# The planned transfer rate, column halves and whole tiles of group 0 in a linear-attention and feed-forward kernel

## Chip, cores and metric

The program runs on one NeuronCore of a Trainium2 chip. The metric is the device time of one execution in microseconds (us); lower is better. Everything is float32 at the interface.

## What is computed

```python
f = 1.0 / (1.0 + np.exp(-f_logit))                     # q, k, v, f_logit: (4, 8, 768, 48)
for t in range(S):
    state = f[:, :, t, :, None] * state + einsum('bhd,bhe->bhde', k[:, :, t], v[:, :, t])
    y[:, :, t] = einsum('bhd,bhde->bhe', q[:, :, t], state)
x = y.transpose(0, 2, 1, 3).reshape(3072, 384)
h = x @ w_in                                           # (384, 2048)
g = h * np.tanh(np.log1p(np.exp(h)))
return g @ w_out                                       # (2048, 384)
```

## The kernel before

**Tiling.** The recurrence is worked chunk by chunk: 24 chunks of 128 time steps of one batch, each by a few small matmuls with a state that is carried along. Four chunks make a group of 512 tokens; there are six groups (g = 0 to 5). The feed-forward part takes a group through 16 tiles of d_ff (j = 0 to 15): `moe_in` gives h of one tile (128 x 512), `mish` turns it into g on ScalarE and VectorE, `moe_out` adds its share to the three output banks o. Groups 0 and 1 are worked in an interleaved order (`units`), so that each half of the weights is loaded once.

**Two precisions of matmul.** As a rule a tile is worked in split form: the operands are split into a high and a low part of type float32r (`split_w`, `split_x`, the last two steps of `mish`), and three products of the parts stand for one, nine matmuls for h (L227) and nine for o (L265). The first tiles of group 0 (j < `WHOLE`) are worked whole instead: plain float32 matmuls, three for h (L235) and three for o (L238), with nothing to split at that point; the weights of such a tile are split later, at its turn in group 1.

**Column halves.** The first `EARLY_J` tiles of group 0 are worked in two halves of 256 tokens: first the halves that need only chunks 0 and 1, then those that need chunks 2 and 3.

**Weights.** The weights of tile j come as one transfer of 768 KB into one of two buffers `raw` (in two pieces of 384 KB each while transfers are "early"), 8 bytes to a pair of numbers, and are put together by L374 on ScalarE and L376, L377, L379 on VectorE. Below, w0 is the weights of tile 0, w2 those of tile 2. A chunk's input comes as two transfers of 512 KB, lk and qv.

**Transfers.** All transfers are issued by SyncE's queue in the order of the plan. The first 32 pieces are paced (`fetch`): each waits until an earlier one has landed, so that at most 1200 KB are under way.

**Order.** Every step is recorded with `Plan.add` (engine, estimated cost in ns, the resources that it reads and writes), and `Plan.order` looks for an order: for each setting (`ahead`, `haste`) it packs the steps by list scheduling, forward and backward in turn, and keeps the packing with the earliest estimated end. `Plan.pack` estimates when a transfer lands: transfers go one after the other at 0.32 KB per ns. Each engine's instructions are then issued in order of their estimated start, and run in that order: an instruction that waits holds up all behind it on its engine. `Plan.issue` fills estimated gaps of TensorE up to the first feed-forward output with matmuls on zeros (L361, `idle`), which count as busy in the profile but compute nothing.

Lines that the steps below touch: L374 to L379 put weights together; L391 and L392 split them; L251, L243, L254, L255 (ScalarE) and L252, L256, L247 (VectorE) are steps of `mish`; L613 and L618 copy a chunk's output and spread the fourth head pair's rows with three matmuls; L503, L517, L476, L560, L572, L584 are the matmuls of the recurrence.

Of the kernel before, what the change touches and what calls it, by code (L numbers as in the profile page):

```python
# [39 lines left out]
PACED = 16  # L40
FLIGHT = 1200
EARLY = 24
EARLY_J = 3
WHOLE = 4


class Plan:
# [26 lines left out]
    def pack(self, rank, ahead, haste, back=False):  # L74


        steps = self.steps
        count = len(steps)
        engine, cost, port = [s[0] for s in steps], [s[1] for s in steps], [s[5] for s in steps]
        before = [s[3] for s in steps]  # L80
        after = [[] for _ in steps]
        for i in range(count):
            for b in before[i]:
                after[b].append(i)
        if back:
            before, after = after, before
        free = dict.fromkeys(self.FREE, 0.0) if back else dict(self.FREE)
        queue = {e: [] for e in free}
        left, ready, start = [len(b) for b in before], [0.0] * count, [0.0] * count
        for i in range(count):  # L90
            if not left[i]:
                queue[engine[i]].append(i)
        transfers = shared = 0.0
        for _ in range(count):
            best = None
            for e, q in queue.items():
                if q:
                    at = [(max(ready[i], shared) if port[i] else ready[i], i) for i in q]
                    t0 = max(free[e], min(at)[0])
                    _, t, i = min(  # L100
                        (rank[i] + haste * max(0.0, r - t0), max(free[e], r), i)
                        for r, i in at if r <= t0 + ahead
                    )
                    if best is None or t < best[0]:
                        best = t, i
            t, i = best
            e = engine[i]
            queue[e].remove(i)
            start[i] = t
            end = free[e] = t + cost[i]  # L110
            if port[i]:
                shared = end
            if e == "sp" and not back:
                transfers = max(transfers, end + 650.0) + steps[i][4] / 0.32
                end = transfers - 650.0
            for a in after[i]:
                f = a if back else i
                if engine[i] == engine[a] == "pe":
                    lag = 0.0
                else:  # L120
                    lag = self.LATENCY[engine[f]]
                    if back and engine[f] == "sp":
                        lag += steps[f][4] / 0.32
                ready[a] = max(ready[a], end + lag)
                left[a] -= 1
                if not left[a]:
                    queue[engine[a]].append(a)
        return start

    def order(self):  # L130
        count = len(self.steps)
        cost = [s[1] for s in self.steps]
        best = None
        for ahead, haste in ((0.0, 0.0), (100.0, 1.0), (100.0, 20.0), (300.0, 20.0), (600.0, 20.0)):
            rank = list(range(count))
            for _ in range(10):
                start = self.pack(rank, ahead, haste)
                end = max(start[i] + cost[i] for i in range(count))
                if best is None or end < best:
                    best, self.start = end, start  # L140
                back = self.pack([-start[i] - cost[i] for i in range(count)], ahead, haste, True)
                rank = [-back[i] - cost[i] for i in range(count)]
        return sorted(range(count), key=lambda i: (self.start[i], i))
# [34 lines left out]
def recurrence_moe_kernel(  # L178
# [89 lines left out]
    with tc.tile_pool(name="work", bufs=1) as pool, tc.tile_pool(  # L268
# [113 lines left out]
        def split_w(j):  # L382
            w, kw = (first[j], ("first", j)) if j < HF else (wt_[j % 2].bitcast(F32), ("wt", j % 2))
            old = [[], []]
            if j >= HF:
                old = [
                    [k for n in held for x in inputs(n)[0] for k in x]
                    + [("s", ("xt", 0, c), t) for c in range(GC) for t in range(NP)],
                    [("first", i) for i in range(HF)],
                ]  # L390
            add("act", T_ACT(W_TILE), lambda: nc.scalar.activation(weights(j)[0], w, AF.Copy), [kw], [("w", "h", j)] + old[0])  # L391
            add("dve", T_DVE(W_TILE), lambda: nc.vector.tensor_tensor(  # L392
                weights(j)[1], w, weights(j)[0].bitcast(F32), ALU.subtract), [kw, ("w", "h", j)],
                [("w", "l", j)] + old[1], port=True)

        def split_x():
            x = xt_[0]
            for a in range(NK):
                ks, kh, kl = ([(z, ("xt", 0, c), a) for c in range(GC)] for z in "shl")
                add("act", T_ACT(GT), lambda a=a: nc.scalar.activation(x[:, 0, a], xs[:, a], AF.Copy), ks, kh)  # L400
                add("dve", T_DVE(GT), lambda a=a: nc.vector.tensor_tensor(
                    x[:, 1, a], xs[:, a], x[:, 0, a].bitcast(F32), ALU.subtract), ks + kh, kl, port=True)
# [256 lines left out]

        units = [(0, j, x) for x in range(2) for j in range(EARLY_J)] + [(0, j, 2) for j in range(EARLY_J, HF)]  # L660
        units += [(1, j, 2) for j in range(HF)] + [(g, j, 2) for g in range(2) for j in range(HF, NF)]
# [3 lines left out]
        def attend_goal(u):  # L665

            per = 4 * GC
            u = u // 2 if u < 2 * EARLY_J else u - EARLY_J
            if u < NF + HF:
# [17 lines left out]
        def out_unit(u):  # L687
# [13 lines left out]
            if u == 0:  # L701
                plan.until = len(plan.steps)
            if g == 0 and j < WHOLE:
                for m in range(NK):
# [26 lines left out]
        for u in range(len(units) + LAG):  # L731
            if u < len(units):
                g, j, part = units[u]
                whole = g == 0 and j < WHOLE
                if g == 0 and part != 1:
                    load_w(j)
                    if not whole:
                        split_w(j)
                if u == EARLY_J + WHOLE:
                    split_x()  # L740
                if g == 1 and j < WHOLE:
                    split_w(j)
# [129 lines left out]
def _layout(q, k, v, f_logit, moe_w_in, moe_w_out):  # L872
# [18 lines left out]
    for a in range(NK):  # L891
        for e in range(2):
            for r in range(16):
                order += [head_at(a, e) * D + 3 * r + m for m in range(3)]
                order.append(head_at(NP - 1, e) * D + 3 * r + a)
    w_in = moe_w_in[np.array(order)].reshape(NK, P, NF, P).transpose(2, 1, 0, 3)
    ww = np.empty((NF, P, 2, NK, P), dtype=moe_w_in.dtype)
    ww[:, :, 0] = w_in
# [33 lines left out]
```

## Time and profile before

| | us |
|---|---|
| median of 3 runs (506.26 to 507.40) | 507.32 |
| profiled execution, its own time | 506.54 |
| its span (first to last instruction) | 504.7 |
| TensorE busy in the span | 490.8 (97%) |
| VectorE, ScalarE, GpSimd busy | 334.7, 356.8, 147.8 |

The profile names PE (TensorE's matmuls), DVE (VectorE), ACT (ScalarE), POOL (GpSimd) and SP (SyncE); L12 is line 12 of the kernel. Two things help in reading it. A plain float32 matmul leaves two records, a float32r one leaves one, so "L235 x6" is three matmuls. And the end of a matmul is modelled and overlaps the start of the next, so that costs of matmuls are best taken from start to start; the same holds in a smaller way on ACT and DVE, where the next instruction starts about 0.1 us before the shown end.

### The profile page before, as it was taken

To read this page: it belongs to the slowest core of one execution; us is meant where nothing else is said; L and a number is where in the kernel's file an instruction comes from. 1 tells how busy PE (TensorE), PEld (TensorE's weight loads), DVE (VectorE), ACT (ScalarE), POOL (GpSimd) and SP (SyncE) were. 2 spreads that over 40 slices of the span, in tenths; PEclk is the share of its full clock that TensorE was granted. 3 is DMA by queue.
4 is the path that set the end of the run, shared out by engine and by line. 5 is a ranking of instruction groups with operands and counts; after the bars stand their busy time and mean duration, and the time that the engine had idled before them with its cause. 6 is when DMAs were issued, how large, how long until landed. Compare 5 with 4: busy or idle time off the path is not lost.

```text
span 504.7 us, 12824 instructions
## 1 busy us (share of the span) xinstructions
PE 490.8 (97%) x5352; PEld 396.0 (78%) x5352; DVE 334.7 (66%) x588; ACT 356.8 (71%) x681; POOL 147.8 (29%) x128
## 2 busy tenths in 40 slices
PE   9779999999999999999999999999999999999995
PEld 8668767788888777787887887888788878878884
DVE  4679999998856874876666756656776453534341
ACT  6769999999976774867667766775776654655561
POOL 0411211100014343344333443443242323332422
PEclk9999999999999999999999999999999999999999
DMA  7875555651300634311221411121230000010001
GB/s 251 266 239 205 196 207 201 218 181 62 126 0 22 202 116 150 113 43 46 83 75 43 147 43 43 64 86 53 83 108 1 2 12 22 24 39 1 0 1 68
DMA packets 17105, 48.47 MB, mean 96 GB/s; under 512 B 2000, under 2 KB 2000, under 8 KB 17040
## 3 DMA queue, kind: packets, MB, share of 16 engines
q1 hardware_dynamic: 17040, 47.59, 27.7%
q8 instruction: 43, 0.70, 0.6%
q14 instruction: 22, 0.18, 0.1%
HBM read 39.32 MB, written 6.29 MB: 90 GB/s over the span
## 4 chain that ended last, share of the span: by engine, by line
PE 82%; DVE 6%; DMA 5%; ACT 4%; issue 1%; SPq 0%; DVEq 0%; ACTq 0%
PE o L265 37%; PE h L227 36%; DMA raw<-ww 3%; PE at L560 2%; PE at L572 2%; DMA in<-qv 2%; PE at L476 2%; PE at L517 2%; PE at L584 1%; DVE wl L392 1%; DVE inv L438 1%; DMA spareh<-qv 1%; ACT wh L391 1%; DMA spareh<-lk 1%; DVE gl L247 0%
## 5 line engine op out<-in xcount | busy, mean ns | idle before, releaser
L248 POOL TENSOR_TENSOR gl<-ng,gh 128x512 fp32r<-128x512 f32 x75 | 104.8, 1400 | 250.2 <-ACT gh L258 156.1
L227 PE MATMUL h<-xt,wh 128*128 128x512 f32 x552 | 173.2, 395 | 0.5 <-DVE ng L256 0.3
L227 PEld LDWEIGHTS h<-xt,wh 128*128 128x128 f32 x552 | 102.4, 188 | 23.6 <-DVE ng L256 0.7
L254 ACT ACTIVATE ng<-ng,half 128x512 f32<-128x512 f32 (+1 forms) x99 | 70.3, 710 | 60.4 <-DVE ng L244 58.1
L265 PE MATMUL o<-gh,wh 128*128 128x512 f32 x276 | 110.5, 400 | 0.0
L265 PE MATMUL o<-gl,wh 128*128 128x512 f32 x276 | 108.2, 392 | 0.0
L227 PE MATMUL h<-xt,wl 128*128 128x512 f32 x276 | 108.1, 392 | 0.0
L265 PE MATMUL o<-gh,wl 128*128 128x512 f32 x276 | 107.8, 391 | 0.0
L256 DVE SCALAR_TENSOR_TENSOR ng<-ng,h 128x512 f32<-128x512 f32 x92 | 63.0, 685 | 57.2 <-ACT ng L255 55.7
L252 DVE TENSOR_SCALAR ng<-ng 128x512 f32<-128x512 f32 (+1 forms) x99 | 49.8, 504 | 57.4 <-ACT ng L251 56.6
L251 ACT ACTIVATE ng<-h 128x512 f32<-128x512 f32 (+1 forms) x99 | 57.7, 583 | 42.1 <-PE h L227 40.6
L258 ACT ACTIVATE gh<-ng 128x512 fp32r<-128x512 f32 x92 | 57.7, 627 | 12.2 <-DVE ng L256 9.8
L255 ACT ACTIVATE ng<-ng 128x512 f32<-128x512 f32 (+1 forms) x99 | 60.7, 613 | 1.5
L265 PEld LDWEIGHTS o<-gh,wh 128*128 128x128 f32 x276 | 51.8, 188 | 11.9
L265 PEld LDWEIGHTS o<-gl,wh 128*128 128x128 f32 x276 | 51.8, 188 | 11.7
L227 PEld LDWEIGHTS h<-xt,wl 128*128 128x128 f32 x276 | 51.8, 188 | 11.7
L265 PEld LDWEIGHTS o<-gh,wl 128*128 128x128 f32 x276 | 51.9, 188 | 10.6
L244 DVE TENSOR_TENSOR ng<-ng 128x512 f32<-128x512 f32 x75 | 53.8, 718 | 2.2
L310 POOL TENSOR_TENSOR in<-in,inv 128x512 f32<-128x512 f32 x20 | 23.9, 1194 | 64.3 <-ACT inv L444 48.2
L438 DVE TENSOR_TENSOR_SCAN inv<-gate,state 128x516 f32<-128x516 f32 x20 | 27.5, 1375 | 8.1 <-ACT gate L429 8.1
L632 DVE TENSOR_TENSOR xt<-at,xt 128x256 fp32r<-128x256 f32 x40 | 16.3, 419 | 11.4 <-ACT xt L631 11.1
L606 POOL TENSOR_TENSOR state<-tmp,ends 128x192 f32<-128x192 f32 x20 | 14.9, 747 | 17.7 <-PE at L560 13.2
(135 smaller groups left out, 520.7 us busy)
## 6 DMA issues: line engine op xcount, KB each, us to landing
raw<-ww SPq DMA_DIRECT2D x12, 768.0 KB, 4.1
in<-lk SPq DMA_DIRECT2D x18, 512.0 KB, 3.6
in<-qv SPq DMA_DIRECT2D x18, 512.0 KB, 3.7
out<-ob SPq DMA_DIRECT2D x18, 256.0 KB, 2.4
raw<-ww SPq DMA_DIRECT2D x8, 384.0 KB, 4.6
in<-lk SPq DMA_DIRECT2D x8, 256.0 KB, 3.8
in<-qv SPq DMA_DIRECT2D x8, 256.0 KB, 4.2
xt<-xt SPq DMA_DIRECT2D x15, 128.0 KB, 2.1
```

The source lines that it names most:

```text
L227: nc.tensor.matmul(h, w[:, a * P : (a + 1) * P], xt[:, x, a, cols], start=(n == 0), stop=(n == 3 * NK - 1))
L244: ("dve", T_DVE(w), 1, lambda: nc.vector.tensor_tensor(n, n, n, ALU.mult))
L248: ("pool", T_POOL(w), 1, lambda: nc.gpsimd.tensor_tensor(gl, g, gh.bitcast(F32), ALU.subtract))
L251: ("act", T_ACT(w, True), 0, lambda: nc.scalar.activation(n, h, AF.Exp)),
L252: ("dve", T_DVE(w / 2), 1, lambda: nc.vector.tensor_scalar(n, n, E_CAP, 1.0, ALU.min, ALU.add)),
L254: ("act", T_ACT(w, False, 1), 0, lambda: nc.scalar.activation(g, n, AF.Ln, bias=half1, scale=0.5)),
L255: ("act", T_ACT(w), 0, lambda: nc.scalar.activation(g, g, AF.Exp, scale=-1.0)),
L256: ("dve", T_DVE(w), 0, lambda: nc.vector.scalar_tensor_tensor(gw if whole else g, g, 1.0, h, ALU.subtract, ALU.mult)),
L258: ("act", T_ACT(w), 0, lambda: nc.scalar.activation(gh, g, AF.Copy)),
L265: nc.tensor.matmul(o, w, x, start=(first and i == 0), stop=(last and i == 2))
L310: add("pool" if on_pool else "dve", cost, lambda: eng.tensor_tensor(dst, x, y, ALU.mult), reads, writes, port=port)
L438: add("dve", 2 * T_DVE(w + st) - 70, lambda s=s, st=st: nc.vector.tensor_tensor_scan(inv1[:, s].rearrange("p a c -> p (a c)"), gate[:, s]. ...
```

## The change

Four numbers and a list. The rate of transfers in the planner goes from 0.32 to 0.27 KB per ns, in both directions of the packing. `EARLY_J` goes from 3 to 2 and `WHOLE` from 4 to 5, so group 0 has two tiles in column halves (0 and 1) and three more in one piece that are whole (2, 3, 4); tile 4 was split before. The planner tries ten settings instead of five, with 30 rounds each instead of 10. No instruction's form changes, and no buffer.

```diff
-EARLY_J = 3
-WHOLE = 4
+EARLY_J = 2
+WHOLE = 5
@@ pack
-                transfers = max(transfers, end + 650.0) + steps[i][4] / 0.32
+                transfers = max(transfers, end + 650.0) + steps[i][4] / 0.27
...
-                        lag += steps[f][4] / 0.32
+                        lag += steps[f][4] / 0.27
@@ order
-        for ahead, haste in ((0.0, 0.0), (100.0, 1.0), (100.0, 20.0), (300.0, 20.0), (600.0, 20.0)):
+        for ahead, haste in ((200.0, 5.0), (400.0, 10.0), (1000.0, 20.0), (200.0, 50.0), (50.0, 2.0), (0.0, 0.0), (100.0, 1.0), (100.0, 20.0), (300.0, 20.0), (600.0, 20.0)):
-            for _ in range(10):
+            for _ in range(30):
```

The built programs show what comes of it. In TensorE's stream 22 zero matmuls (L361) stand instead of 27; split-form matmuls fall from 828 to 819 each for h and o, and whole ones of 512 tokens rise from 3 to 9 each, those of 256 tokens fall from 18 to 12 each.

The first place is the third load of weights, w2. On ScalarE before, its copy L374 stands ahead of the copy L613 of chunk 3's output (`spareh<-at`):

```order
L444 ACTIVATE inv_84<-inv_84 128x4x128
L243 ACTIVATE ng_92<-ng_92 128x256
L374 ACTIVATE wt_102<-raw_100 128x768
L613 ACTIVATE spareh<-at_105 128x128
L254 ACTIVATE ng_92<-ng_92,half_68 128x256
L451 ACTIVATE ends<-at_106 128x4
```

and now:

```order
L613 ACTIVATE spareh<-at_105 128x128
L613 ACTIVATE spareh<-at_104 128x2x128
L451 ACTIVATE ends<-at_106 128x4
L251 ACTIVATE ng_92<-h_108 128x256
L429 ACTIVATE gate_83<-gate_83,ones 128x4x128
L400 ACTIVATE xt_90<-spareh 128x512
L243 ACTIVATE ng_92<-ng_92 128x256
L251 ACTIVATE ng_92<-h_107 128x256
L506 ACTIVATE kt_85<-at_106 128x512
L374 ACTIVATE wt_102<-raw_100 128x768
L254 ACTIVATE ng_92<-ng_92,half_68 128x256
```

Chunk 3's copies and several others have moved ahead of w2's copy; behind it stands a step of `mish` (L254) of tile 1's first half. On VectorE now, w2's next two steps stand ahead of that half's last step (L256 on h_108):

```order
L401 TENSOR_TENSOR xt_90<-spareh,xt_90 128x512
L376 TENSOR_SCALAR wt_102<-wt_102 128x768
L543 TENSOR_TENSOR mid_88<-state,at_106 128x64x3
L377 SCALAR_TENSOR_TENSOR wt_102<-raw_100,wt_102 128x768
L256 SCALAR_TENSOR_TENSOR ob_93<-ng_92,h_108 128x256
```

L256 was behind the same two steps before, for the first half of tile 0 (h_107); which half it is has moved on by one.

The second place is TensorE at the end of chunk 3. Before, up to the first recurrence matmuls of chunk 4:

```order
L361 MATMUL o_111<-state_74 128x128 x2
L618 MATMUL at_104<-spareh,sparel 128x128 x2
L618 MATMUL at_105<-spareh,sparel 128x128
L503 MATMUL at_106<-ident,in_81 128x128 x4
L361 MATMUL o_111<-state_74 128x128 x4
L517 MATMUL at_106<-in_81,kt_85 48x16x3 x2
```

and now:

```order
L235 MATMUL h_108<-spareh,sparel 128x256 x3
L618 MATMUL at_104<-spareh,sparel 128x128 x2
L618 MATMUL at_105<-spareh,sparel 128x128
L238 MATMUL o_111<-ob_93,sparel 128x256
L238 MATMUL o_110<-ob_93,sparel 128x256
L235 MATMUL h_107<-spareh,sparel 128x256 x3
L503 MATMUL at_106<-ident,in_81 128x128 x4
L238 MATMUL o_109<-ob_93,sparel 128x256
L517 MATMUL at_106<-in_81,kt_85 48x16x3 x2
```

The zero matmuls are gone here and whole matmuls of the feed-forward part (L235, L238) stand between. The next L235 block, on h_108 again (tile 1's second half), follows behind chunk 4's L517 and L476.

The third place is SyncE's queue, w0 and w1 first (raw_100 and raw_101 of 128x768), w4 (raw_100 of 128x1536) below:

```order
 L347 DMA in_82<-lk 128x512 x2
 L347 DMA spareh<-lk 128x512 x4
-L347 DMA raw_100<-ww 128x768 x2
 L347 DMA in_82<-qv 128x512 x2
 L347 DMA spareh<-qv 128x512 x2
+L347 DMA raw_100<-ww 128x768 x2
+L347 DMA spareh<-qv 128x512 x2
 L347 DMA raw_101<-ww 128x768 x2
-L347 DMA spareh<-qv 128x512 x2
...
+L347 DMA in_81<-lk 128x1024
 L347 DMA raw_100<-ww 128x1536
-L347 DMA in_81<-lk 128x1024
```

w0 moved behind the inputs of chunks 1 and 2, w1 behind those of chunk 3; the pieces ahead of w2 are the same as before in sum. w4 moved behind the first input of chunk 6.

## Rows read from the trace of the kernel before

**Rows 1.** Busy time by stretch, all engines (columns in the first line)

```profile
core 0: us, PE busy (x) PEld busy (x) DVE busy (x) ACT busy (x) POOL busy (x), PEclk, DMA share, GB/s
5.00:35.00 30.00, 24.68 (x620) 20.99 (x618) 18.67 (x35) 20.80 (x50) 7.83 (x8) 1.00 0.85 273
...
35.00:40.00 5.00, 4.00 (x30) 3.78 (x34) 3.29 (x6) 4.55 (x12) 0.00 (x0) 0.66 0.28 89
40.00:60.00 20.00, 20.00 (x363) 15.46 (x358) 19.76 (x41) 19.71 (x49) 5.23 (x4) 1.00 0.59 208
...
80.00:100.00 20.00, 19.72 (x226) 15.84 (x225) 19.93 (x34) 17.84 (x33) 1.99 (x3) 1.00 0.64 216
```

**Rows 2.** Waits of TensorE: instruction, releaser, us in total, times, longest

```profile
PE at L618 <- ACT spareh L613: 2.6, 1, 2.6
PE h L572 <- issue: 1.2, 1, 1.2
...
PE h L227 <- DVE ng L256: 0.3, 1, 0.3
PE h L227 <- DVE ob L256: 0.3, 1, 0.3
```

**Rows 3.** Chain of work that ended last, 28 to 38 us: start, us, what

```profile
31.27 3.54 DMA raw<-ww
...
34.89 0.89 ACT wt L374
35.78 0.18 ACT spareh L613
...
36.00 1.34 PE at L618 x6
```

**Rows 4.** Timeline of TensorE: start, us, line, operation, shapes, records

```profile
15.32 0.85 PE L618 MATMUL at<-spareh,sparel 128*128 128x128 f32 x6
...
37.99 1.92 PE L361 MATMUL o<-state 128*128 128x128 f32 x8
...
42.22 1.03 PE L238 MATMUL o<-ob,sparel 128*128 128x256 f32 x4
43.08 1.46 PE L235 MATMUL h<-spareh,sparel 128*128 128x256 f32 x6
...
53.49 2.84 PE L235 MATMUL h<-spareh,sparel 128*128 128x512 f32 x6
56.27 0.45 PE L584 MATMUL at<-ident,in 48*128 48x48 f32 x8
```

**Rows 5.** Timeline of VectorE behind the landing of w2

```profile
35.81 0.56 DVE L376 TENSOR_SCALAR wt<-wt 128x768 int32<-128x768 int32 x1 [3.29 <-ACT wt L374]
36.29 0.28 DVE L252 TENSOR_SCALAR ng<-ng 128x256 f32<-128x256 f32 x1
36.49 0.95 DVE L377 SCALAR_TENSOR_TENSOR wt<-raw,wt 128x768 int32<-128x768 int32 x1
37.36 0.41 DVE L256 SCALAR_TENSOR_TENSOR ob<-ng,h 128x256 f32<-128x256 f32 x1
37.69 0.95 DVE L379 SCALAR_TENSOR_TENSOR sparel<-raw,wt 128x768 int32<-128x768 int32 x1
...
40.69 0.33 DVE L543 TENSOR_TENSOR mid<-state,at 128x192 f32<-128x192 f32 x1
```

**Rows 6.** Chain of work that ended last, 65 to 98 us

```profile
65.11 2.37 PE h L227 x9
...
93.83 0.61 DVE ng L256
...
94.48 2.34 PE h L227 x9
96.82 2.06 PE o L265 x9
```

**Rows 7.** Timeline of the queue of SyncE: issue of w4

```profile
38.70 0.33 SPq L347 DMA_DIRECT2D raw<-ww  x1
```

## The prediction

> **What bounds the kernel now.** I read the busy times by stretch first, then TensorE's waits, then the chain of work and the timelines at the one long wait. TensorE is busy all the time from 40 us on, or nearly so: 20.00 of 20 us and 19.72 of 20 in the stretches shown [rows 1]. So the end comes when TensorE's work has been fed through, and only three things can move it: idle time (mostly before 40 us), zero matmuls, and the amount of work. From 5 to 35 us TensorE is busy 24.68 of 30 us, at a DMA rate of 273 GB/s [rows 1]: there it waits for data. The list of waits has one that stands out, 2.6 us in one piece, on ScalarE's copy L613 [rows 2]; the others are 1.2 us and less. The chain shows what is behind it: a piece of weights (w2) lands at 34.81 (31.27 + 3.54), its copy L374 runs at 34.89, the copy L613 of chunk 3's output comes only behind it at 35.78, and TensorE's L618 starts at 36.00 [rows 3]. L613 needs nothing of w2: it is held up because ScalarE works in order and L374 was queued ahead. The plan had reckoned with 0.32 KB per ns; the trace shows 0.273. After that wait the granted clock is 0.66 on average from 35 to 40 us, against 1.00 from 5 to 35 [rows 1], and four zero matmuls take 1.92 us at half clock [rows 4]. So between 33.4 us (36.00 less 2.6) and 39.9 us (37.99 + 1.92) TensorE does next to nothing: that is what the change can win.
>
> **The new rate and order.** The pieces ahead of w2's last one are the same in sum, and all are paced, so I take its landing at 34.81 again. In the new order chunk 3's copies stand ahead of w2's L374, so L618 and what follows no longer wait for w2. Something else does: on VectorE, w2's L376, then L543 and L377, stand ahead of L256 of tile 1's first half, and TensorE's next L235 on the same bank (tile 1's second half) must wait until that L256 has read it. The time of that L235, step by step: L376 starts at 35.81 as before and takes 0.48 to the next start [rows 5]; L543 takes 0.26 (0.33 shown at 40.69, less 0.07 of overlap, as L376 shows 0.56 and takes 0.48); L377 takes 0.87 (36.49 to 37.36); L256 takes 0.41; TensorE starts 0.04 later, as at 35.96 to 36.00 [rows 3, 5]. 35.81 + 0.48 + 0.26 + 0.87 + 0.41 + 0.04 = **37.87 us**. ScalarE has three activations in a row behind L374 (to 35.78) before that L256 may start at 37.41, 1.6 us; each has a third of L374's columns (0.89 us, [rows 3]), so an estimated 0.4 us, and they don't set it.
>
> TensorE must also have got there. To that point it has to do, beyond what it had done by 33.4 us before: L618 (0.85 us, [rows 4] at 15.32), L503 (at most 0.65, from 37.34 to 37.99 at partly half clock [rows 3, 4]), L517 and L476 (1.0: from 39.91 to 42.22 less one L235 block of 1.30), three matmuls of L235 and three of L238 of 256 columns at 0.43 each (0.86 for two, 42.22 to 43.08 [rows 4]), 2.6 in all, less one zero matmul, 0.2. That is 4.9 us, so it arrives by 38.3 us even if all idle time before 33 us stays. Some of that should go, since chunk 1's inputs land earlier (w0 went behind them) and w0's and w1's copies no longer stand in front of others; I expect TensorE to arrive between 36 and 37.5 and to idle for up to 1.9 us. The ends are 37.87 and 38.3; I take 37.87.
>
> How far ahead is that? Before, the same amount of work is done when L517, L476, the L235 block and three matmuls of L238 are: two of those end at 43.08, the third 0.43 later, 43.51 us [rows 4]. The **lead is 43.51 - 37.87 = 5.64 us** (5.2 at the other end). It holds the wait, the zero matmuls and the half clock together, so none of them counts again.
>
> By a rule of the Trainium skill the transfers themselves would not bound this stretch so: the page DMA: Bandwidth & Descriptors, Specifications, gives about 358 GB/s from HBM for a core. By that w2 would land at an estimated 27 us, the new plan's rate would be too low rather than right, and the lead would be up to 2 us more; the trace has 273 GB/s, so the sum goes by 34.81 us.
>
> **One more whole tile.** Tile 4 in whole form is three matmuls of 512 columns for h and three for o. At 0.43 us for 256 columns, one of 512 takes 0.86, a block of three 2.58. In split form a block of nine takes 2.06 [rows 6]. So 0.52 us more, twice: **+1.04 us** on the path, since TensorE is full there. The shown blocks bound it: 2.78 for a whole one (53.49 to 56.27 [rows 4]) against 2.34 or 2.06 [rows 6], so +0.9 to +1.4. Its split (L391, L392) moves to group 1, and its L258 and L247 go: relief for ScalarE and VectorE early, nothing for TensorE. **Two tiles in halves instead of three** costs TensorE nothing (512 columns at 0.86 either way) and saves ScalarE and VectorE some overhead per instruction. The ten settings and 30 rounds run when the program is built; only their order counts.
>
> **Later waits.** Two waits of 0.3 us, at 65.11 and 94.48, are left on TensorE behind VectorE [rows 2, 6]. VectorE has less to do ahead of the second: eight instructions fewer stand ahead of that L256 (93.83) in the new order, three of a weight tile (L377, L379, L392) at 0.87, two of 512 columns (L247, L726) at about 0.61, two halves of L252 at 0.20, and the L256 themselves 0.05 less, 4.3 us in all; it also idles less before 37 us, since L376's wait of 3.29 us [rows 5] now has other work in front. I take both waits as gone: -0.6 (0 at the other end).
>
> **Sum:** -5.64 + 1.04 - 0.6 = **-5.2 us**. The profiled execution took 506.54 us, so 501.3. The median of the runs shown is 0.8 higher, which would give 502.1; I forecast the middle, **501.7 us**. With every term at its better or its worse end the sum is -5.3 or -3.8, which is 501.6 or 503.1 from the same middle.
>
> **Rivals.** *The clock falls again.* Before, TensorE stood idle for 2.6 us and then the granted clock was at its lower level, 1.2 GHz, for 3.4 us (0.66 over 5 us) [rows 1, 2]. An idle time of 1.2 us earlier did not do that: the clock is 1.00 from 5 to 35 us. The new wait before 37.87 lies between, 0 to 1.9 us. If the clock falls, real work stands there now, so 3.4 us at half clock cost 1.7 us: **503.4 us**. The Trainium skill, TensorE: Matmul & The Clock Gate, Part 1: The HAM clock gate, says that idling throttles the clock and that the moment varies from run to run; the first part agrees with the trace, the second no run here shows.
>
> *VectorE becomes the bound.* It is busy 19.76 of 20 us and 19.93 of 20 [rows 1], and the chain comes to TensorE at 94.48 through it [rows 6]. If its idle time does not shrink, it is only 4.3 us earlier at 93.83, which holds TensorE to that: 506.9 (the middle) less 4.3, 502.6. If waits of 0.3 to 0.5 us come up at four tiles of group 0, 503.8. I take **503.2 us**.
>
> *The change does not do what it says.* w2 lands later, or another conversion stands where w2's stood. Each us later at 37.87 costs one; from 41.5 us on (w2 landing at 38.4) nothing is left that could be told from no change: **506 us**. Against it: the pieces ahead of w2 are the same in sum.
>
> *The weights of the next tiles come late, and it is slower.* w4 goes into w2's buffer, which L379 frees. Before, that ends at 38.64 and w4 is issued at 38.70 [rows 5, 7]. Now L379 stands behind L256, five more VectorE instructions and their waits, and ends near 41, so w4 is issued some 2.3 us later; the two buffers hand that on. If TensorE had to wait 2.3 us each for w4, w5 and w6, 6.9 us, the sum turns to +1.7: **508.6 us**. It decides from about 2.2 us at each of the three. Against it: no wait for weights is in TensorE's list, and between 37.87 and w4's first use stand an estimated 15 us of TensorE's work (two whole tiles' L235, one tile's L238, three pieces of chunks), while from 41 on the transfer needs about 3.5 [rows 3] and the four conversion steps about 3 [rows 3, 5].
>
> **Chances.** Forecast 0.48, clock 0.28, VectorE 0.13, no effect 0.06, late weights 0.05. The first three are faster by over 0.3% (1.5 us, about what a measurement of this kernel can tell from no change), but for a tail of 0.02: faster 0.87, same 0.08, slower 0.05. For 8 in 10 the range takes the forecast's own nearly whole, the clock and VectorE: **500.7 to 504.6 us**.
>
> **What would show it.** The profile after should have no wait of L618 on L613 near 36 us; a wait of L235 on VectorE's L256 (`ob`) of at most 2 us ending at 37.9; no zero matmuls after 30 us; the first L227 of group 1 some 5 us earlier; nine L235 of 512 columns. A granted clock under 1 between 36 and 42 us would show the first rival; waits of L227 or L265 on VectorE between 60 and 115 us the second; a wait behind `raw<-ww` after 45 us the last. The forecast is wrong if the L235 after chunk 4's L476 starts later than 39 us, or if TensorE idles for more than 1.5 us in all after it.

## The result, and the profile after

The changed kernel takes **503.4 us** (median of 6 runs, 502.3 to 504.3) against 506.83 (6 runs, 505.64 to 507.4) for the kernel before on the same chip: a ratio of 0.9915, 95% interval 0.9895 to 0.9936, so 0.6 to 1.1% faster. That is the ratio on record; the quotient of the two medians is 0.9932, inside the interval. The profiled execution took 503.37 us, its span 501.6 (before 506.54 and 504.7). The forecast was 501.7, with 500.7 to 504.6 as its range; 503.4 is also what the first rival gave.

All of TensorE's waits after, which answer to [rows 2] (instruction, releaser, us in total, times, longest):

```profile
PE h L235 <- DVE ob L256: 2.6, 1, 2.6
PE o L361 <- DVE state L325: 1.1, 1, 1.1
PE at L517 <- ACT ends L451: 0.8, 1, 0.8
PE h L235 <- ACT ends L451: 0.5, 1, 0.5
PE at L517 <- ACT kt L506: 0.3, 1, 0.3
```

The wait of L618 on L613 is gone, and so are the two of L227. In its place stands one of the same length at L235, behind VectorE. The 1.1 us at L361 lies at the start and was there before as well.

Busy time by stretch, with the columns of [rows 1]:

```profile
5.00:35.00 30.00, 28.57 (x640) 24.29 (x638) 19.49 (x39) 24.19 (x62) 8.93 (x8) 1.00 0.81 258
...
35.00:40.00 5.00, 2.16 (x69) 1.92 (x70) 3.78 (x9) 4.31 (x10) 0.38 (x1) 1.00 0.78 271
40.00:45.00 5.00, 5.00 (x97) 3.57 (x96) 4.67 (x8) 3.77 (x10) 1.35 (x2) 0.66 0.38 116
```

TensorE is busy for 28.57 us from 5 to 35 us where it was for 24.68, at a lower DMA rate, 258 GB/s for 273. The low granted clock, 0.66, has moved from 35:40 to 40:45. From 60 to 100 us TensorE is busy for all of the 40 us; before, 0.25 and 0.28 were missing.

The chain of work that ended last, 28 to 44 us (start, us, what), beside [rows 3]:

```profile
28.01 4.64 DMA in<-qv
...
32.67 3.13 DMA raw<-ww
...
35.89 0.91 ACT wt L374
...
36.82 0.07 DVE wt L376
...
37.29 0.35 DVE mid L543
37.64 0.87 DVE wt L377
38.51 0.34 DVE ob L256
...
38.90 1.68 PE h L235 x6
40.58 1.71 PE o L238 x4
```

The steps are those of the prediction, one by one, but w2 lands at 35.80 (32.67 + 3.13), not at 34.81, and all that follows is 1.0 us later. TensorE's timeline from there (start, us, line, shapes, records, idle time before and its releaser):

```profile
35.64 0.66 PE L476 MATMUL at<-in 48*64 48x64 f32 x32
38.90 1.68 PE L235 MATMUL h<-spareh,sparel 128*128 128x256 f32 x6 [2.60 <-DVE ob L256]
40.37 1.91 PE L238 MATMUL o<-ob,sparel 128*128 128x256 f32 x4
...
44.39 2.84 PE L235 MATMUL h<-spareh,sparel 128*128 128x512 f32 x6
47.17 0.57 PE L517 MATMUL at<-in,kt 64*48 64x48 f32 x32
...
59.33 2.84 PE L238 MATMUL o<-ob,sparel 128*128 128x512 f32 x6
61.60 1.02 PE L227 MATMUL h<-xt,wh 128*128 128x512 f32 x2
```

Two matmuls of L238 take 1.84 us here (40.37 to 42.21, the start of L584), against 0.86 before [rows 4]: half clock, on real work.

### The profile page after: what moved, and what is told of

The parts are those of the page before. It is cut to its first block, busy times and chain, and to the rows that moved or that the text cites. A ratio compares the mean times of both kernels' runs of the same rounds, so it can differ in the third digit from the quotient of the medians.

```text
span 501.6 us, 12770 instructions
## 1 busy us (share of the span) xinstructions
PE 490.3 (98%) x5324; PEld 391.1 (78%) x5324; DVE 333.4 (66%) x585; ACT 356.9 (71%) x677; POOL 148.6 (30%) x127
## 4 chain that ended last, share of the span: by engine, by line
PE 91%; DMA 6%; DVE 1%; ACT 0%; issue 0%; SPq 0%; DVEq 0%; ACTq 0%
PE o L265 38%; PE h L227 38%; PE o L238 3%; PE at L560 3%; PE at L572 2%; PE h L235 2%; PE at L517 2%; PE at L476 2%; DMA spareh<-qv 2%; PE at L584 1%; DMA raw<-ww 1%; DMA in<-lk 1%; DMA in<-qv 1%; DMA spareh<-lk 1%; ACT wt L374 0%
## 5 line engine op out<-in xcount | busy, mean ns | idle before, releaser
L248 POOL TENSOR_TENSOR gl<-ng,gh 128x512 fp32r<-128x512 f32 x74 | 103.1, 1395 | 251.5 <-ACT gh L258 157.7
L227 PE MATMUL h<-xt,wh 128*128 128x512 f32 x546 | 171.8, 396 | 0.0
L227 PEld LDWEIGHTS h<-xt,wh 128*128 128x128 f32 x546 | 101.5, 188 | 23.1 <-issue 0.7
L254 ACT ACTIVATE ng<-ng,half 128x512 f32<-128x512 f32 (+1 forms) x98 | 69.9, 713 | 59.7 <-DVE ng L244 57.4
L265 PE MATMUL o<-gl,wh 128*128 128x512 f32 x273 | 106.8, 391 | 0.0
L227 PE MATMUL h<-xt,wl 128*128 128x512 f32 x273 | 106.7, 391 | 0.0
L265 PE MATMUL o<-gh,wl 128*128 128x512 f32 x273 | 106.7, 391 | 0.0
L256 DVE SCALAR_TENSOR_TENSOR ng<-ng,h 128x512 f32<-128x512 f32 x91 | 62.4, 686 | 57.0 <-ACT ng L255 55.5
L255 ACT ACTIVATE ng<-ng 128x512 f32<-128x512 f32 (+1 forms) x98 | 60.4, 616 | 1.4
L227 PEld LDWEIGHTS h<-xt,wl 128*128 128x128 f32 x273 | 51.2, 188 | 11.8
L310 POOL TENSOR_TENSOR in<-in,inv 128x512 f32<-128x512 f32 x20 | 26.0, 1298 | 55.2 <-ACT inv L444 37.5
```

Of the source, the lines that this page charges most:

```text
L227: nc.tensor.matmul(h, w[:, a * P : (a + 1) * P], xt[:, x, a, cols], start=(n == 0), stop=(n == 3 * NK - 1))
L248: ("pool", T_POOL(w), 1, lambda: nc.gpsimd.tensor_tensor(gl, g, gh.bitcast(F32), ALU.subtract))
L254: ("act", T_ACT(w, False, 1), 0, lambda: nc.scalar.activation(g, n, AF.Ln, bias=half1, scale=0.5)),
L255: ("act", T_ACT(w), 0, lambda: nc.scalar.activation(g, g, AF.Exp, scale=-1.0)),
L256: ("dve", T_DVE(w), 0, lambda: nc.vector.scalar_tensor_tensor(gw if whole else g, g, 1.0, h, ALU.subtract, ALU.mult)),
L265: nc.tensor.matmul(o, w, x, start=(first and i == 0), stop=(last and i == 2))
```

## Experiments

Each comparison is with the kernel before, run on the same chip beside it; its median was 508.84 us beside e1 to e4, 508.49 beside c1 and e5 to e7, and 508.26 beside the others (1.4 to 2.0 us more than in the result above, so ratios count, not times). The ratios are those on record; the quotients of the medians differ from them by up to 0.0022 (e7: 0.9931).

| kernel | median, us | ratio, 95% interval |
|---|---|---|
| e1, rate alone | 506.90 | 0.9969 (0.9947 to 0.9991) |
| e2, tiles alone | 507.39 | 0.9979 (0.9960 to 0.9998) |
| e3, rate and settings, old tiles | 506.21 | 0.9953 (0.9934 to 0.9972) |
| e4, rate and tiles, old settings | 505.09 | 0.9920 (0.9892 to 0.9947) |
| c1, changed kernel again | 503.77 | 0.9898 (0.9868 to 0.9929) |
| e5, w2 behind tile 1's first half | 502.76 | 0.9894 (0.9857 to 0.9930) |
| e6, the wait filled | 503.77 | 0.9910 (0.9879 to 0.9942) |
| e7, 2000 KB under way | 504.97 | 0.9909 (0.9877 to 0.9942) |
| e8, before with w2's copy moved | 507.29 | 0.9979 (0.9956 to 1.0002) |
| e9, rate 0.26 | 502.31 | 0.9890 (0.9852 to 0.9928) |
| e5 a second time | 502.61 | 0.9882 (0.9848 to 0.9915) |
| c2, changed kernel a third time | 503.99 | 0.9915 (0.9885 to 0.9945) |

### Which part brings it: e1 to e4

**e1**, the new rate in the kernel before (both places):

```diff
-                transfers = max(transfers, end + 650.0) + steps[i][4] / 0.32
+                transfers = max(transfers, end + 650.0) + steps[i][4] / 0.27
```

> Theory (the rate): the gain comes from where w2's copy L374 stands on ScalarE. In this order it stands behind chunk 3's copies L613, as in the changed kernel, so TensorE's wait of 2.6 us at L618 should be gone and a shorter one on VectorE's L256 should be the longest near 37 to 39 us; there is no further whole tile to pay for (1.04 us). Expected 503.0 to 505.5 us, 1.3 to 3.8 faster than before, and a resume of TensorE between 37.5 and 39.5 us. Rival (the tiles): what counts is that whole tiles give TensorE work while w2 is on its way; then this kernel is within 0.3% of before (505.3 to 508.3), with zero matmuls or idle time of some 3 us left near 36 us.

It is 0.3% faster, less than expected for the place of the copy. The wait of L618 is gone, as expected; but TensorE resumes at 41.10 us, not between 37.5 and 39.5. Its chain of work:

```profile
31.98 5.26 DMA raw<-ww
...
37.33 0.92 ACT wt L374
...
40.17 0.88 DVE sparel L379
...
41.10 1.58 PE h L235 x6
```

This L235 (idle 1.19 us before it) waits for the whole of w2's conversion, L379 included: it is tile 2's first half, which stands fourth among the halves in TensorE's order. With three tiles in halves TensorE needs w2 itself there. In the changed kernel the wait goes on L256 and not on L379, and tile 2 comes at 44.39. e1 also has waits later on, up to 1.4 us at L227 (67.02), where the clock falls.

**e2**, the new tiles at the old rate:

```diff
-EARLY_J = 3
-WHOLE = 4
+EARLY_J = 2
+WHOLE = 5
```

> Theory (the rate): L374 of w2 still stands ahead of L613 of chunk 3 here, so ScalarE holds TensorE up until w2 has landed (some 35 us): a wait of 1.5 us or more near 36 us stays, and the tile adds 1.04 us: 505.5 to 508 us, no faster than before by over 0.3%. Rival (the tiles): the two tiles in halves and five whole ones bring the gain at the old rate too: 503 to 505 us, with no wait over 1 us between 33 and 40 us.

0.2% faster, about as the theory had it: the copy L374 of w2 still stands ahead of L613, and TensorE waits for it, 1.35 us (expected: 1.5 or more). The chain of work, then TensorE's timeline:

```profile
35.83 0.89 ACT wt L374
36.72 0.17 ACT spareh L613
```

```profile
36.94 0.94 PE L618 MATMUL at<-spareh,sparel 128*128 128x128 f32 x6 [1.35 <-ACT spareh L613]
```

**e3**, the changed kernel with `EARLY_J` 3 and `WHOLE` 4:

> New rate and new settings with the old tiles. Here the order that the planner takes puts L374 of w2 ahead of chunk 3's last copies L613 again, but the transfer of w2 itself two pieces earlier (512 KB, at the 273 KB per us of before an estimated 1.9 us, so a landing near 33 us). Theory (the place of the copy): a wait of TensorE behind L613 comes back, but shorter, some 0.5 to 1.5 us, and five zero matmuls stand near it: 504 to 506 us. Rival (the tiles): without them most of the gain is lost, 505.5 to 508. Rival (the settings): they bring it, 502.5 to 503.9.

0.5% faster. The expected wait came, but one step further on: w2 lands at 34.50, the last copies L613 and chunk 4's copy L506 stand behind its L374, and TensorE waits 0.92 us for L506 at L517 (0.5 to 1.5 were expected, right behind L613). The chain of work:

```profile
29.61 4.89 DMA raw<-ww
...
34.58 0.91 ACT wt L374
35.49 0.45 ACT spareh L613 x2
35.94 0.50 ACT kt L506
```

TensorE's timeline shows zero matmuls on both sides of it:

```profile
33.83 1.73 PE L361 MATMUL o<-state 128*128 128x128 f32 x14
36.48 0.57 PE L517 MATMUL at<-in,kt 64*48 64x48 f32 x32 [0.92 <-ACT kt L506]
36.87 0.66 PE L476 MATMUL at<-in 48*64 48x64 f32 x32
37.46 1.60 PE L361 MATMUL o<-state 128*128 128x128 f32 x12
38.90 1.46 PE L235 MATMUL h<-spareh,sparel 128*128 128x256 f32 x6
```

Thirteen zero matmuls stand ahead of this L235, some 3.2 us; the changed kernel has none after 28 us, and works at tile 0's second half (L235, 32.56) ahead of chunk 4's L517. Earlier, at 18.13, e3 waits 1.96 us for chunk 1's input.

**e4**, the changed kernel with five settings and ten rounds:

> New rate and new tiles with five settings and ten rounds. L374 of w2 stands behind chunk 3's copies L613. Theory (the rate and the place of the copy): no wait of L618 on L613; about the changed kernel's time, 502.5 to 505 us; three zero matmuls ahead of chunk 4 may cost half a us of that. Rival (the settings): the ten settings found what the others cannot find, and this one is within 0.3% of before, 505.3 to 508.3 us.

0.8% faster, as the changed kernel is within the intervals (0.9915, 0.9898, 0.9915). L235 waits 1.83 us behind L256 at 40.23, much as there; here w2, which lands at 36.90, is in the way.

So neither the rate nor the tiles do it alone (0.3% and 0.2%); both together bring 0.8%, and for the settings nothing is left that these runs can tell. That the two together bring more than their sum is likely, not shown: the two ratios multiplied are 0.9948, at the edge of e4's interval, and have an interval of their own. The rate takes w2's copy out of the way of chunk 3's copies, and with two tiles in halves TensorE's next block there needs no w2. The second point is the one that the prediction did not see. `EARLY_J` and `WHOLE` were always changed together, so that it is the halves and not the fifth whole tile is read from the traces (e1 above, e8 below), not from a run of its own.

### The wait that took the place: e5, e7, e8

**e5**, the changed kernel with w2's copy behind tile 1's first half's L255 on ScalarE, and w2's L376 and L377 behind that half's L256 on VectorE. `plan.at` notes a step's number; the moves act on the finished order:

```diff
-        return sorted(range(count), key=lambda i: (self.start[i], i))
+        out = sorted(range(count), key=lambda i: (self.start[i], i)); [(out.remove(a), out.insert(out.index(b) + 1, a)) for a, b in self.moves]; return out
...
+        m, w = plan.at["mish", 1], plan.at["w", 2]; plan.moves = [(w, m + 4), (w + 2, m + 5), (w + 1, m + 5)]
```

> The changed kernel with three instructions moved: w2's copy L374 stands behind the last ScalarE step (L255) of tile 1's first half, and w2's L376 and L377 behind that half's L256 on VectorE. Theory (the wait is w2's place in two queues): nothing ahead of that L256 waits for w2 any more, so the L235 that started at 38.90 starts between 36.6 and 37.2, after an idle time of under 1 us, and the clock stays at 1.00. Up to 2.0 us and 1.7 us of clock could come of it; part is given back, since what comes next (L584 behind GpSimd and ScalarE, tile 2's weights) is not earlier: 1 to 2.5 us faster than the changed kernel of this call. Rival (w2 is needed anyway): the time comes back as a wait for tile 2's weights, within 0.3% of it.

```profile
37.06 1.56 PE L235 MATMUL h<-spareh,sparel 128*128 128x256 f32 x6 [0.41 <-DVE ob L256]
38.46 1.03 PE L238 MATMUL o<-ob,sparel 128*128 128x256 f32 x4
40.40 0.45 PE L584 MATMUL at<-ident,in 48*128 48x48 f32 x8 [0.91 <-POOL in L310]
```

TensorE's timeline shows the wait of L235 down to 0.41 us, as expected, so its cause was w2's place in the two queues; and 0.91 us of it comes back two blocks later, at L584 behind GpSimd. Net, that is 1.85 - 0.41 - 0.91 = 0.5 us less waiting than in c1.

> The kernel with w2's copy and its next two steps behind tile 1's first half once more, since 1.0 us between two medians of six runs does not settle which is faster. If the move is worth what the profiles show (TensorE's first whole tile of 512 columns at 42.0 instead of 44.2 to 44.4 us, its end 1.3 to 2.0 us earlier), it is 0.7 to 1.5 us faster than the changed kernel of this call; if the rest gives it back, within 0.5 us of it.

Its two medians are 1.0 and 1.4 us under those of the changed kernel run beside it (502.76 and 503.77; 502.61 and 503.99). The intervals against before overlap; run by run, 10 of its 12 are under 503.43 us, and 2 of the changed kernel's 13. It is the faster of the two in these runs, by more than the 0.5 us of waits; neither of its two profiles has a fall of the clock before TensorE's last matmul, which may be the rest, but that isn't shown.

**e7**, the changed kernel with more under way, the order the same:

```diff
-FLIGHT = 1200
+FLIGHT = 2000
```

> The changed kernel with 2000 KB under way at most instead of 1200, the order unchanged. Theory (the pacing sets the rate of 258 GB/s from 5 to 35 us): the rate there rises to 280 or more, w2 lands 1 to 3 us before 35.8, the wait of L235 shrinks by as much: 1 to 3 us faster than the changed kernel of this call. Rival (the memory or the queues set the rate): the rate stays within 10 GB/s of 258, w2 lands within 0.5 us of 35.8, and the time is within 0.3%, or up to 1 us slower if pieces needed first share the rate with later ones.

The rate from 5 to 28 us is 339 GB/s; in the changed kernel it is 263. First e7, then the changed kernel:

```profile
5.00:28.00 23.00, 20.30 (x505) 17.68 (x504) 11.60 (x26) 16.27 (x40) 5.91 (x6) 0.96 0.97 339
28.00:35.00 7.00, 7.00 (x124) 5.75 (x123) 5.28 (x10) 4.65 (x13) 1.15 (x1) 0.90 0.25 63
```

```profile
5.00:28.00 23.00, 22.04 (x552) 19.14 (x550) 12.90 (x30) 17.86 (x45) 5.89 (x6) 1.00 0.82 263
```

So the pacing sets the rate, as the theory had it: w2's pieces, issued at 23.55 for 29.31, were in well before ScalarE came to them. But the gain did not follow. The wait of L235 is still there:

```profile
41.52 1.56 PE L235 MATMUL h<-spareh,sparel 128*128 128x256 f32 x6 [1.85 <-DVE ob L256]
```

This settles what the wait is made of. It does not end at a time that w2's landing fixes: it follows TensorE. On ScalarE, L374 stands behind chunk 4's copy L506, which needs TensorE's own L503, and ahead of L254, L243 and L255, the first and last of them steps of tile 1's first half. However early w2 is, L374's 0.9 us and VectorE's L376 and L377 lie between L503 and the next L235. c1, where w2 was in time too, shows the same 1.85 us, and c2 1.84. Only in the first profile of the changed kernel did the landing add to it (2.60). In the median e7 takes 1.2 us more than c1, with intervals that overlap. Its profile has a wait of 1.94 us inside a block of L572 at 25.63 for which it names no releaser ("issue"), with a fall of the clock behind it; whether the higher rate has to do with that stays open.

**e8**, the kernel before with w2's copy behind chunk 4's L506, on ScalarE alone:

```diff
-        plan.idle = idle
+        plan.idle = idle; plan.moves = [(plan.at["w", 2], plan.at["kt", 4])]
```

> The kernel before with one instruction moved: w2's copy L374 stands on ScalarE behind chunk 4's copy L506, and so behind chunk 3's copies L613; nothing else moves, no rate, no tile. Theory (the wait of 2.6 us was the place of this copy): no wait of L618 on L613 is left, L618 starts near 33.5 instead of 36.0, the next wait is that of L235 on VectorE's L256 behind w2's L376 and L377, until 37.5 to 38.5 (before, that L235 started at 40.82): 1 to 3 us faster than before. Rival (several orders meet the same limit): what is gained at L618 is waited for again at L235 and behind, within 0.3% of before.

In this kernel w2's L376 and L377 stand ahead of the copy in the program, so they leave out the wait for it and work on what the buffer held before: tile 2's weights come out wrong, and VectorE doesn't wait for the copy until L379. The time is thus, if anything, that of a kernel with less waiting.

```profile
37.47 1.56 PE L235 MATMUL h<-spareh,sparel 128*128 128x256 f32 x6 [1.31 <-DVE sparel L379]
39.93 1.46 PE L235 MATMUL h<-spareh,sparel 128*128 128x256 f32 x6
```

L618's wait is gone, the next one is 1.31 us on w2's L379 (tile 2's first half again), and TensorE is at the block of 43.08 [rows 4] at 39.93, 3.15 us ahead, more than expected. Part is given back behind it: 1.2 us of waits at L227 on L256, 0.6 before. Its span is 2.0 us shorter in the profiled execution, which was its fastest; in the median 1.0 us are left, and the interval reaches 1.0002. So moving the copy alone is worth 0.2% here, which can't be told from nothing: as the rival had it.

### The clock: e6, c1, c2

**c1 and c2** are the changed kernel, unchanged.

> The changed kernel once more, beside the three kernels of this call that build on it. Theory: the wait of L235 on VectorE's L256 (2.6 us) and a granted clock under 1 between 40 and 45 us come again, since both follow from the order. Rival: the fall of the clock is a matter of the moment and is missing here. The time should be 0.985 to 0.995 of before either way.

> The changed kernel a third time, for the comparison of this call. Theory (the clock falls behind a wait, but behind which one is a matter of the execution): the granted clock is under 1 for some 3.4 us once, behind the wait of L235 or behind an earlier one, and not behind both. Rival: it falls behind the wait of L235 again whenever that is over 1.5 us. 0.987 to 0.994 of before.

Busy time by stretch, c1 and then c2:

```profile
5.00:35.00 30.00, 27.39 (x629) 23.43 (x628) 17.57 (x36) 22.19 (x58) 8.31 (x8) 0.94 0.83 257
40.00:45.00 5.00, 4.75 (x100) 3.72 (x101) 4.64 (x10) 4.41 (x11) 1.76 (x2) 1.00 0.39 109
```

```profile
5.00:35.00 30.00, 27.59 (x628) 23.72 (x626) 17.46 (x35) 22.16 (x59) 7.96 (x8) 0.94 0.81 255
40.00:45.00 5.00, 4.41 (x18) 3.32 (x18) 4.67 (x11) 4.20 (x10) 1.18 (x1) 0.66 0.37 111
```

One program, three profiles: the granted clock falls at 40 us in the first, behind a wait of 2.60 us; in c1 before 35 us, behind a wait of 1.35 us inside a block of L572 at 21.25, and not behind the 1.85 us of L235; in c2 at both places, behind 1.9 and 1.8 us. So the theory for c1 (the same place again) is wrong and its rival (a matter of the moment) right; the theory for c2 (not twice) is wrong, and c1 speaks against c2's rival (always behind a wait over 1.5). Which wait the fall follows is a matter of the execution. The Trainium skill, TensorE: Matmul & The Clock Gate, Part 1: The HAM clock gate, says of the rise at the start of a kernel that its moment varies from run to run. These three profiles show it of the fall; no run had shown it before the prediction.

What a fall costs can be read from c1 and the first profile, from that L235 to the first block of 512 columns:

```profile
40.25 1.56 PE L235 MATMUL h<-spareh,sparel 128*128 128x256 f32 x6 [1.85 <-DVE ob L256]
...
44.23 1.12 PE L235 MATMUL h<-spareh,sparel 128*128 128x512 f32 x2
```

3.98 us at full clock, 5.49 (38.90 to 44.39) with the fall: **1.5 us**. In c2 the same stretch takes 5.66 us (40.59 to 46.25), 1.7 more.

**e6**, the changed kernel with chunk 4's scores done five times over:

```diff
-                    score(e, c, p) for p in range(NP) for e in range(2) for c in range(2)], ["kt", kv[0]] + reads,
+                    score(e, c, p) for _ in range(5 if n == GC else 1) for p in range(NP) for e in range(2) for c in range(2)], ["kt", kv[0]] + reads,
```

> The changed kernel, in which chunk 4's score matmuls (L476) are done five times over instead of once, the same values each time: some 2.4 us of work that nobody needs in the wait of 2.6 us, at four blocks of 0.59 us. Theory (the clock falls because TensorE stood idle): the wait shrinks to 0.2 us or so, the next L235 starts at 38.9 as before, the granted clock stays 1.00 from 40 to 45 us, and the kernel is 1.7 us faster than the changed kernel of this call (half of 3.4 us). Rival (the clock falls for another reason, or these small matmuls count for nothing): the clock falls as before, within 0.3% of it; slower by 0.3 us at most.

```profile
36.78 2.53 PE L476 MATMUL at<-in 48*64 48x64 f32 x160
39.32 1.81 PE L235 MATMUL h<-spareh,sparel 128*128 128x256 f32 x6
```

The wait is filled, and the clock is 1.00 from 40 to 45 us, as the theory expects; but the median is that of c1 (503.77 both), and the 1.7 us that it expects are not there. With c1 at 1.00 there as well, one profile of e6 proves nothing on the clock; and the filled stretch is as long as the wait was (L235 starts 2.94 us behind L517, in c1 2.91). The run is inconclusive.

### Is 0.27 the right rate: e9

```diff
-                transfers = max(transfers, end + 650.0) + steps[i][4] / 0.27
+                transfers = max(transfers, end + 650.0) + steps[i][4] / 0.26
```

> The changed kernel with the planner's rate at 0.26 KB per ns instead of 0.27, nearer to the 257 to 261 GB/s that the profiles since the change show. Its order differs from the changed kernel's in many places (w0 and w1 stand ahead of one more input each, two more copies stand ahead of w2's L374). Theory (a rate that fits the trace makes the plan better): 0.988 to 0.993 of before. Rival (the plan's end is one lucky order among several of about the same plan): 0.994 to 1.000 of before, with other waits of 1 us and more.

0.9890 of before, with another order and hardly a wait (0.7 us the longest after the start): as good as the changed kernel or better (502.31 and 503.99 side by side, intervals overlapping). So 0.27 is not one lucky value, though no other new rate was tried. Nor is the rate a constant that one could read off: with 0.26 in the plan the trace shows 270 GB/s from 5 to 35 us, with 0.27 it shows 258, 257 and 255.

## Why the prediction held, and which steps of it failed

| step | predicted | profiled after |
|---|---|---|
| w2's landing | 34.81 | 35.80 |
| L235 of tile 1's second half | 37.87 | 38.90 |
| lead on 43.51 | 5.64 | 4.61 |
| half clock on real work | 0 (rival: 1.7) | 1.5 |
| one more whole tile | 1.04 | 0.93 |
| later waits | -0.6 | -0.53 |
| sum | -5.2 | -2.7; the span is 3.1 shorter |

**What held.** L618's wait went, L235 behind VectorE's L256 took its place, and the chain of six steps behind w2 took 3.10 us (35.80 to 38.90) for the 3.06 worked out. The whole tile's price is 2.78 (44.39 to 47.17) and 2.27 for its o block, less twice 2.06 [rows 6]. Of the signs named, L235 started by 39 us (38.90), TensorE has no listed wait behind it, and no zero matmul stands after 30 us; but the wait was 2.6 us and not at most 2, and the clock was under 1 between 36 and 42 us, the first rival's sign. The two later waits are gone, so the rival of VectorE is out; no wait behind `raw<-ww` came, so that of late weights is out; and the change does what it says. 0.4 us between the sum and the span are not accounted for.

**What was mis-sized: w2's landing.** "The pieces ahead of w2's last one are the same in sum, and all are paced, so I take its landing at 34.81 again": the bytes were the same, the rate wasn't (258 for 273 GB/s), and it cost 1.0 us of the lead. Why the new order has the lower rate under the same pacing stays open.

**What failed: the idle time.** The prediction took the wait to end at a fixed time, so that TensorE, arriving at 36 to 37.5, would idle for at most 1.9 us, and could idle less by arriving later. It arrived at 36.30 and idled for 2.60. c1 and e7 show that arriving later doesn't help: 1.85 us is what the order itself makes, however early w2 is, and the landing added the other 0.75. So the clock rival, with its wait of "0 to 1.9 us", was in truth one with 1.85 us or more, and it came about: 1.5 us by rows, for the 1.7 forecast. The forecast and its rival differ by just the 1.7 us that the result lies above the forecast, so the range held because it took the rival in. In c1 the clock fell elsewhere, and the time was lost there.

**What was left out: the halves.** "Two tiles in halves instead of three costs TensorE nothing": true of its matmuls, but e1 and e8 show that it decides when w2 is needed. Without it the gain is 0.3 to 0.5%. The prediction came out near the mark because it read the order of the changed kernel as it stood, where both edits were at work.

**The median against the profile.** Between the medians of all executions beside the experiments the gain is 4.5 us (508.47 over 60 of before, 503.99 over 13 of the changed kernel), where the two spans differ by 3.1. Every execution's record holds its mean granted clock: 0.991 in the mean (0.983 to 0.999) for before, 0.995 (0.991 to 0.997) for the changed kernel. Among those at 0.997 and more, before has 505.40, 506.41 and 506.55 us, the changed kernel 502.65, 503.31 and 503.43: 3.1 us between the middle ones. So the rest seems to go along with the clock. But that is three executions each, and the mean also takes in the last microseconds of the span, in which TensorE has nothing left to do: from 500 to 502 us the clock is 0.50 in the first profile of the changed kernel and 1.00 in that of before. The profiled execution of e9, in which it did not fall under work, has a mean of 0.997, that of before, in which it did, 0.996: the mean hardly tells them apart. That fewer waits mean fewer falls is a reading, not shown.

## What to carry to other kernels

An engine that works in order makes everything behind an instruction wait for that instruction's data, so ask for each copy of a late transfer what stands behind it on its engine, and then who needs the transfer itself first: here both had to be moved, 0.8% together for 0.3% and 0.2% alone. When a wait sits behind another engine's queue, see whether it ends at a fixed time or follows the waiting engine's own work; in the second case earlier data shorten it only down to what the order makes (1.85 us here), and the rest takes another order. Take three profiles before a term of some 1.5 us is put down to a place: in three profiles of this one program the clock fell at different waits.

## What the runs showed of the hardware

**The DMA rate followed the pacing.** With 1200 KB under way it is 263 GB/s from 5 to 28 us, with 2000 KB and the same order 339. At 1200 KB it is 271 in the kernel before and 249 to 263 in three profiles of the changed one, so the order seems to move it too, by less. The prediction set the 358 GB/s of the Trainium skill, DMA: Bandwidth & Descriptors, Specifications, against the 273 of the trace and went by the trace; that was right for this kernel. e7 shows that the two don't contradict each other: from 10 to 24 us, with the DMA engines busy all the time, it moves 360 GB/s.

**Falls of the clock.** While TensorE has work left, 8 of the 14 profiles show one (c2 two), each behind a wait of 1.0 us or more; single waits of 1.85 (c1, e7) and 1.96 us (e3) passed without.

**Waits without a releaser.** In 8 of the 14 profiles TensorE stands still for 0.3 to 1.9 us, mostly in the middle of a block of L572, and the profile names nothing that it waits for; the others, the first of the changed kernel among them, have none. What it is stays open.
